# Attention's value rows fetched once on 32 partitions, with GpSimd copying them to the other 96

## The chip, the cores and the metric

The kernel runs on one core of a Trainium2 chip. The metric is the device time of one execution in microseconds (us), the median of several runs. A profile of one further execution shows when each instruction ran on each engine: PE (TensorE, matrix multiplies, with PEld its weight loads), DVE (VectorE), ACT (ScalarE), POOL (GpSimd) and SP (SyncE, which here issues nearly all DMAs). SBUF is the on-chip memory with 128 partitions, PSUM the accumulator memory of PE, DRAM the memory outside.

## What is computed

Attention with a bias that depends on position, followed by a gated feed-forward block, all in float32:

```python
B, H, S, D = q.shape                      # 8, 8, 576, 64
scores = 1/sqrt(D) * q @ k^T + bias       # bias: [H, S, S], a small MLP of the relative position
attn   = softmax(scores)                  # max subtracted, 1e-9 added to the sum
x      = attn @ v                         # then heads side by side: [B*S, H*D] = [4608, 512]
out    = ((x @ w1) * (x @ w2)) @ w3 @ w_out
```

`w3` is 1024 by 1024 and `w_out` 1024 by 512. The inputs of the feed-forward block arrive as 64-bit floats and are converted to float32 on the chip.

## The kernel before

There are three stages. A prologue computes the bias and writes it to DRAM. The attention stage runs from about 60 to 490 us. The feed-forward stage takes the rest.

**Units.** Attention works through 32 units: four pairs of heads times eight batches. For each unit, `op_S` multiplies queries and keys (nine tiles of 128 query rows, L264), `op_T` adds the bias, takes the row extreme and scales on DVE (L275), `op_E` takes the exponential on ACT (L304), `op_R` transposes 32 by 32 blocks on DVE into the tile `pt` (L314), `op_W` multiplies the transposed probabilities with the values (L360), and `op_X` empties PSUM on ACT (L369, L374).

**Why the values stand four times.** A 32-by-32 block transpose leaves the probabilities of a block of 32 keys spread over four groups of 32 partitions, each group holding other query rows. `op_W` therefore contracts over 32 partitions at a time, with `rows = slice(32 * a, 32 * a + 32)` for a = 0 to 3, and needs the same 32 value rows on each of the four groups. Before the change the host repeats them four times in DRAM, and `op_l` (DMA at L252) loads all 128 partitions. A unit's values come as five parts `v0` to `v4` of 4, 4, 3, 4 and 3 key blocks. Each part has one buffer, so part n of the next unit is loaded only after `op_W` of part n in this unit has read it.

**The order of work.** The functions `rhythm` and `arrange` hold a table of times per unit, with a period of 12.17. Work is sorted by these numbers, and this fixes the instruction order on PE, ACT, DVE and POOL. The order on SP's DMA queue is made by the framework's scheduler from the dependences. Every engine executes its own instructions strictly in order, and so does SP: a DMA whose condition is not met holds back all DMAs behind it.

**What else runs beside attention.** In units 1 to 6 of each eight, one block of feed-forward weights is converted, 24 blocks in all, in seven steps `c0` to `c6`: fetch into the tile `wi` (SP, L140), three passes on ACT (`c1` L145, `c2` L149, `c3` L152), a clamp on POOL (`c4`, L155), a shift on DVE (`c5`, L159) and two POOL instructions that put the result together (`c6`, L163 and L164). `wi` has two buffers. The fetch of a later block waits for the L164 that last read its buffer.

In units 2 to 6 of each eight, for the first three pairs of heads, the bias tiles `nb0`, `nb1`, `nb4`, `nb5` and `nbM` of the next pair are loaded from DRAM by `load_bias` (L233; L224 and L225 for `nbM`). POOL first writes zeros to one column of the tile (L230, L223), and the DMA waits for that write.

Of the kernel before, what the change touches and what calls it, by code (L numbers as in the profile page):

```python
# [42 lines left out]
def rhythm(tiles, turns):  # L43

    at = {}
    for n, t in enumerate(tiles):
        at["S" + t] = S_AT[n], "PE"
        at["T" + t] = T_AT[n], "DVE"
        at["E" + t] = E_AT[n], "ACT"
    for n, ts in enumerate(turns):  # L50
        at["R" + ts] = R_AT[n], "DVE"
    at["r"] = PERIOD + 2.62, "DVE"
    at["rd"] = PERIOD + 3.80, "SP"
    for n, w in enumerate(W_AT):
        at[f"W{n}"] = PERIOD + w, "PE"
        at[f"lv{n}"] = w + 1.90, "SP"
    at["X"] = 2 * PERIOD + 1.70, "ACT"
    at["xd"] = 2 * PERIOD + 2.80, "SP"
    for h in range(2):
        for k, n in enumerate("kq"):  # L60
            at[f"l{n}{h}"] = -2 * PERIOD + (5.50, 9.80)[h] + 0.1 * k, "SP"
    at["c0"] = 0.2, "SP"
    at["c1"] = 5.60, "ACT"
    at["c2"] = 8.15, "ACT"
    at["c3"] = 11.65, "ACT"
    at["c4"] = 6.30, "POOL"
    at["c5"] = 9.20, "DVE"
    at["c6"] = 12.40, "POOL"
    return at


def arrange(NU, pieces):

    at = [rhythm(FIRST, ("02", "13", "46", "57", "M"))]
    at += [rhythm(TILES, ("02", "46", "M", "13", "57")) for u in range(1, NU)]
    for k, n in enumerate(("lk0", "lq0")):
        at[2][n] = -2 * PERIOD + 9.60 + 0.1 * k, "SP"
    return {
        (n, u): (u * PERIOD + t + 1.4, e) for u in range(NU) for n, (t, e) in at[u].items() if n[0] != "c" or u in pieces
    }  # L80
# [3 lines left out]
def relpos_attention_moe(  # L84
# [17 lines left out]
    nc = tc.nc  # L102
    NPAIR, B, _, S2 = q.shape
    S, D, H = S2 // 2, P // 2, 2 * NPAIR
# [102 lines left out]
    st = {u: {} for u in range(NU)}  # L207
# [31 lines left out]
    def op_l(u, which):  # L239
        p, b = units[u]  # L240
        n = int(which[1])
        if which[0] == "v":
            b0, b1 = PARTS[n]
            t = vp.tile([P, b1 - b0, 2, D], F32, name=f"v{n}")
            src = v[p, b].rearrange("p (b h d) -> p b h d", h=2, d=D)[:, b0:b1]
            for i in range(b0, b1):
                st[u]["v", i] = t[:, i - b0]
        else:
            w = S if which[0] == "q" else HS
            t = st[u][which] = raw.tile([P, w], F32, name=which)  # L250
            src = {"q": q, "k": k}[which[0]][p, b][:, n * w:(n + 1) * w]
        nc.sync.dma_start(t, src)  # L252

    def op_S(u, t):

        d = st[u]
        s = d["s", t] = ps_s.tile([P, 2, 512], F32, name="s")
        for hf, rows in enumerate((lo, hi)):
            if t == "M":
                parts = [(outs, g, 512, 64) for g, outs in enumerate((lo, hi))]  # L260
            else:
                parts = [(slice(0, P), int(t) % 2, int(t) // 2 * P, P)]
            for outs, h, q0, n in parts:
                nc.tensor.matmul(  # L264
                    s[outs, hf, :HS], d[f"q{h}"][rows, q0:q0 + n],
                    d[f"k{h}"][rows, :], start=True, stop=True,
                )
# [18 lines left out]
    for i in range(2):  # L286
        t = att.enter_context(tc.tile_pool(name=f"sums{i}", bufs=1)).tile([P, 64], F32, name=f"sums{i}")
# [105 lines left out]
    def op_c(u, n):  # L393
        pieces[u][int(n)]()

    made = dict(l=op_l, S=op_S, T=op_T, E=op_E, R=op_R, r=op_r, W=op_W, X=op_X, x=op_x, c=op_c)
    later = []
    for (n, u), (at, on) in arrange(NU, pieces).items():
        step = lambda n=n, u=u: made[n[0]](u, n[1:])
# [13 lines left out]
    with ExitStack() as pro:  # L413
# [29 lines left out]
        def reach(G):  # L443

            return (G + 1) * GR - 1, S - 1 - G * GR
# [9 lines left out]
        for G in range(NGRP):  # L455
            n = max(reach(G)) + 1
# [42 lines left out]
        for G in range(NGRP):  # L499
            at = -LEAD + G * PACE_B  # L500
# [162 lines left out]
    for i in range(2 * NF):  # L663
        at = t_s + AT_F + min(i, N_F) * PACE_F0 + max(i - N_F, 0) * PACE_F
# [11 lines left out]
    for n in range(4, 2 * NF):  # L676
        at = t_s + AT_W1 + PACE_W * n
# [10 lines left out]
    for n in range(NCH * NF):  # L688
        c, ft = divmod(n, NF)
        at = t_f + STEP * n  # L690
# [62 lines left out]
```

## Time and profile before

| | us |
|---|---|
| median of 3 runs (1141.06 to 1141.1) | 1141.07 |
| the profiled execution | 1142.65 |
| its span, first to last instruction | 1140.9 |
| stretch 60 to 480: DVE busy | 392.38 of 420 |
| stretch 60 to 480: PE busy | 385.36 of 420 |
| stretch 60 to 480: ACT busy | 307.75 of 420 |
| stretch 60 to 480: POOL busy | 111.34 of 420 |

In the stretch 60 to 480 the 16 DMA engines are busy 0.71 of the time and move 226 GB/s on average. From 480 us on they are busy 0.18 of the time. Busy times of PE are modelled ends, so a busy PE is not a PE at its peak. A row of the timeline gives start, duration, engine, line, operation and tiles, and in brackets how long the engine was idle before and what ended that. "issue" there means that the engine waited for nothing that the profile shows.

### The profile page before, as it was taken

To read this page: it belongs to the slowest core of one execution; us is meant where nothing else is said; L and a number is where in the kernel's file an instruction comes from. 1 tells how busy PE (TensorE), PEld (TensorE's weight loads), DVE (VectorE), ACT (ScalarE), POOL (GpSimd) and SP (SyncE) were. 2 spreads that over 40 slices of the span, in tenths; PEclk is the share of its full clock that TensorE was granted. 3 is DMA by queue.
4 is the path that set the end of the run, shared out by engine and by line. 5 is a ranking of instruction groups with operands and counts; after the bars stand their busy time and mean duration, and the time that the engine had idled before them with its cause. 6 is when DMAs were issued, how large, how long until landed. Compare 5 with 4: busy or idle time off the path is not lost.

```text
span 1140.9 us, 32065 instructions
## 1 busy us (share of the span) xinstructions
PE 1086.7 (95%) x13696; PEld 801.6 (70%) x13696; DVE 637.3 (56%) x1204; ACT 510.2 (45%) x1111; POOL 179.9 (16%) x167
## 2 busy tenths in 40 slices
PE   7988999899899989898999999999999999999998
PEld 2355666566565655576888888888888888888887
DVE  8999899899998989846552212222131312223111
ACT  7867767677776767656442121121212112121212
POOL 0023303330331133334440000000000000000000
PEclk9989999899999999999999999999999999999999
DMA  8958676786777667455231202021121202110100
GB/s 277 309 186 287 221 233 219 243 260 214 243 252 252 184 206 226 138 147 159 70 115 38 73 23 68 21 72 40 52 59 37 56 19 74 38 38 1 37 1 37
DMA packets 100558, 149.04 MB, mean 131 GB/s; under 512 B 22848, under 2 KB 53696, under 8 KB 100416
## 3 DMA queue, kind: packets, MB, share of 16 engines
q1 hardware_dynamic: 99984, 146.98, 40.7%
q8 instruction: 107, 1.75, 0.6%
q14 instruction: 35, 0.29, 0.1%
q10 hardware_dynamic: 432, 0.02, 0.0%
HBM read 116.93 MB, written 30.03 MB: 129 GB/s over the span
## 4 chain that ended last, share of the span: by engine, by line
PE 71%; DVE 16%; issue 7%; DMA 2%; ACT 2%; SPq 1%; POOL 0%; DVEq 0%; ACTq 0%; POOLq 0%
PE up L623 35%; PE o L648 17%; PE acc L360 8%; DVE pt L314 7%; PE s L264 7%; DVE ts L275 6%; PE bacc L485 3%; PE wacc L582 1%; DVE zdve L471 1%; ACT x L369 1%; DVE mx L275 1%; DMA nb<-nb_d 0%; DMA rb<-r_m 0%; DVE wmag L159 0%; DMA x_d<-x 0%
## 5 line engine op out<-in xcount | busy, mean ns | idle before, releaser
L631 DVE TENSOR_TENSOR g<-up,a 128x512 f32<-128x512 f32 x72 | 49.8, 692 | 343.7 <-PE up L623 343.7
L360 PE MATMUL acc<-pt,v 32*64 32x128 f32 (+1 forms) x9216 | 214.7, 299 | 27.1 <-issue 19.5
L304 ACT ACTIVATE pp<-ts,mx 128x576 f32<-128x576 f32 x256 | 197.0, 770 | 91.0 <-DVE mx L275 89.8
L360 PEld LDWEIGHTS acc<-pt,v 32*64 32x64 f32 x9216 | 162.4, 133 | 95.4 <-issue 64.8
L623 PE MATMUL up<-xh,wl 128*128 128x512 f32 x576 | 225.1, 391 | 0.0
L623 PE MATMUL up<-xl,wh 128*128 128x512 f32 x576 | 225.1, 391 | 0.0
L623 PE MATMUL up<-xh,wh 128*128 128x512 f32 x576 | 225.1, 391 | 0.0
L264 PE MATMUL s<-k,q 64*128 64x288 f32 (+1 forms) x1280 | 200.0, 450 | 10.6 <-DVE mx L275 4.9
L275 DVE CUSTOM_DVE_ANT_0 ts<-s,nb 128x576 f32<-128x576 f32 x256 | 183.2, 739 | 27.4 <-PE s L264 26.6
L648 PE MATMUL o<-w3s,gh 128*128 128x512 f32 x576 | 177.7, 390 | 0.0
L314 DVE STREAM_TRANSPOSE pt<-pp 128x1152 f32<-128x1152 f32 x128 | 175.7, 1373 | 0.0
L628 ACT COPY a<-up 128x512 f32<-128x512 f32 x72 | 42.2, 587 | 263.0 <-PE up L623 263.0
L264 PEld LDWEIGHTS s<-k,q 64*128 64x128 f32 (+1 forms) x1280 | 93.9, 180 | 81.0 <-DVE mx L275 35.6
L623 PEld LDWEIGHTS up<-xl,wh 128*128 128x128 f32 x576 | 108.2, 188 | 23.4
L623 PEld LDWEIGHTS up<-xh,wl 128*128 128x128 f32 x576 | 108.2, 188 | 23.4
L623 PEld LDWEIGHTS up<-xh,wh 128*128 128x128 f32 x576 | 108.2, 188 | 23.3
L648 PEld LDWEIGHTS o<-w3s,gh 128*128 128x128 f32 x576 | 108.1, 188 | 22.9
L634 ACT ACTIVATE gh<-g 128x512 fp32r<-128x512 f32 x72 | 45.5, 632 | 173.7 <-DVE g L631 173.7
L648 PE MATMUL o<-w3s,gl 128*128 128x512 f32 x288 | 112.1, 389 | 0.0
L609 POOL TENSOR_SCALAR xh<-xr 128x512 fp32r<-128x512 f32 x36 | 22.5, 624 | 446.6 <-DVE xr L605 445.7
L155 POOL TENSOR_SCALAR wmag<-wmag 128x512 f32<-128x512 f32 x24 | 46.0, 1915 | 243.3 <-ACT wmag L145 243.3
L637 DVE TENSOR_TENSOR gl<-g,gh 128x512 fp32r<-128x512 f32 x72 | 50.8, 705 | 51.3 <-ACT gh L634 51.2
(68 smaller groups left out, 906.6 us busy)
## 6 DMA issues: line engine op xcount, KB each, us to landing
v<-in_v_dram SPq DMA_DIRECT2D x96, 256.0 KB, 4.5
q<-in_q_dram SPq DMA_DIRECT2D x64, 288.0 KB, 4.7
wi<-in_moe_w_dram SPq DMA_DIRECT2D x32, 512.0 KB, 4.3
v<-in_v_dram SPq DMA_DIRECT2D x64, 192.0 KB, 4.1
nb_d<-bev SPq DMA_DIRECT2D x36, 295.5 KB, 4.8
k<-in_k_dram SPq DMA_DIRECT2D x64, 144.0 KB, 3.7
nb<-nb_d SPq DMA_DIRECT2D x16, 576.0 KB, 5.6
x_d<-x SPq DMA_DIRECT2D x32, 288.0 KB, 5.1
```

The source lines that it names most:

```text
L155: clamps.tensor_scalar(d["mag"], d["mag"], LEAST, MOST, op0=ALU.max, op1=ALU.min)
L264: nc.tensor.matmul(s[outs, hf, :HS], d[f"q{h}"][rows, q0:q0 + n], d[f"k{h}"][rows, :], start=True, stop=True,)
L275: nc.vector.tensor_tensor_reduce(out=halves(ts), in0=d.pop(("s", t))[:, :, :HS], in1=halves(NB[p, t]), op0=ALU.add, op1=ALU.min, scale=-1. ...
L304: nc.scalar.activation(d["p", ps][:, k * S:(k + 1) * S], ts, AF.Exp, bias=mx, scale=-1.0, accum_out=SUMS[u // 4 % 2][:, col:col + 1],)
L314: nc.vector.transpose(o, st[u].pop(("p", ts)))
L360: nc.tensor.matmul(acc[outs, a, c0:c0 + 32 * (t1 - t0)], d["v", b][rows, h], pt_[rows, t0:t1, 32 * b:32 * b + 32], start=(b == 0), stop=(b ...
L623: nc.tensor.matmul(acc, l[:, cc], r, start=(n == 0), stop=(n == 3 * NC - 1))
L628: nc.scalar.copy(a, ps[0])
L631: nc.vector.tensor_tensor(g, ps[1], a, op=ALU.mult)
L634: nc.scalar.activation(gh, g, AF.Copy)
L637: nc.vector.tensor_tensor(gl, g, f(gh), op=ALU.subtract)
L648: nc.tensor.matmul(d["o", t], l[:, sl], folded[ft][:, r], start=(ft == 0 and n == 0), stop=(ft == NF - 1 and n == 2),)
```

## The change

Three things change. The host no longer repeats the value rows four times. `op_l` loads each value part into partitions 0 to 31 only, so that a part of four blocks is 64 KB instead of 256 KB, and one of three blocks 48 KB instead of 192 KB. A new step `op_V` makes two POOL copies per part: partitions 0 to 31 to 32 to 63, then 0 to 63 to 64 to 127. The second copy waits for the first. The table gives `op_V` of part n the time w + 5.50, where w is the part's entry in `W_AT`, and it moves `c5` from 9.20 to 9.30.

```diff
         at[f"lv{n}"] = w + 1.90, "SP"
+        at[f"V{n}"] = w + 5.50, "POOL"
...
-    at["c5"] = 9.20, "DVE"
+    at["c5"] = 9.30, "DVE"
...
             for i in range(b0, b1):
                 st[u]["v", i] = t[:, i - b0]
+            st[u]["vt", n] = t
+            t = t[0:32]
...
         nc.sync.dma_start(t, src)
+
+    def op_V(u, n):
+
+        t = st[u].pop(("vt", int(n)))
+        nc.gpsimd.tensor_copy(t[32:64], t[0:32])
+        nc.gpsimd.tensor_copy(t[64:128], t[0:64])
...
-    inputs["v"] = _np.tile(a.reshape(*a.shape[:3], -1), (1, 1, 4, 1))
+    inputs["v"] = a.reshape(*a.shape[:3], -1)
```

The lines of the changed kernel stand a few lines further down: L155 is L156 there, L159 is L160, L163 and L164 are L164 and L165, L252 is L255, L275 is L284, and the two copies are L260 and L261.

**POOL, third pair of heads, units 2 and 3 of eight.** Before, two clamps (L155) stand with the two closing instructions (L163, L164) between them, and the zero column of `nb1` follows the second clamp:

```order
L155 TENSOR_SCALAR wmag_5253<-wmag_5253 128x512
L163 TENSOR_TENSOR w3s2_70<-w3s2_70,wmag_5253 128x512
L164 TENSOR_TENSOR w3s2_70<-w3s2_70,wi_5251 128x512
L155 TENSOR_SCALAR wmag_5509<-wmag_5509 128x512
L230 MEMSET nb1_5645 128x1
L163 TENSOR_TENSOR w3s3_71<-w3s3_71,wmag_5509 128x512
L164 TENSOR_TENSOR w3s3_71<-w3s3_71,wi_5507 128x512
```

Now, from behind the first of these L164 (and the copies of part 2) on:

```order
L260 COPY v3_5662<-v3_5662 32x512
L261 COPY v3_5662<-v3_5662 64x512
L260 COPY v4_5711<-v4_5711 32x384
L261 COPY v4_5711<-v4_5711 64x384
L156 TENSOR_SCALAR wmag_5693<-wmag_5693 128x512
L231 MEMSET nb1_5835 128x1
L260 COPY v0_5767<-v0_5767 32x512
L261 COPY v0_5767<-v0_5767 64x512
L260 COPY v1_5827<-v1_5827 32x512
L261 COPY v1_5827<-v1_5827 64x512
L164 TENSOR_TENSOR w3s3_71<-w3s3_71,wmag_5693 128x512
L165 TENSOR_TENSOR w3s3_71<-w3s3_71,wi_5691 128x512
```

The clamp now stands behind the copies of parts 3 and 4, and the closing pair stands behind those of parts 0 and 1.

**DVE, at the shift `c5` of the next unit.** `ppM` is the ninth tile of probabilities, the odd one. Before:

```order
L275 ISA ts_5935,mx_5936<-s_5904,nb5_4179 128x576
L275 ISA mx_5936 128x1
L159 TENSOR_SCALAR wmag_5765<-wmag_5765 128x512
L314 STREAM_TRANSPOSE pt0_841<-ppM_5893 128x576
L275 ISA ts_5955,mx_5956<-s_5939,nb5_4179 128x576
```

Now:

```order
L284 ISA ts_6137,mx_6138<-s_6104,nb5_4311 128x576
L284 ISA mx_6138 128x1
L323 STREAM_TRANSPOSE pt0_841<-ppM_6093 128x576
L160 TENSOR_SCALAR wmag_5959<-wmag_5959 128x512
L284 ISA ts_6157,mx_6158<-s_6141,nb5_4311 128x576
```

The shift and the transpose of `ppM` have changed places. Nothing else moves on DVE, and PE and ACT keep their order.

**SP, third pair of heads, units 5 and 6.** Before, the loads of `nb5` and `nbM` (two DMAs) stand ahead of `v0` and of the fetch of `wi`:

```order
L233 DMA nb5_6211<-nb_d_87 128x2x576
L252 DMA v0_6097<-in_v_dram 128x512
L252 DMA k0_6106<-in_k_dram 128x288
L252 DMA q0_6141<-in_q_dram 128x576
L252 DMA v1_6155<-in_v_dram 128x512
L252 DMA v2_6204<-in_v_dram 128x384
L252 DMA k1_6202<-in_k_dram 128x288
L252 DMA q1_6206<-in_q_dram 128x576
L224 DMA nbM_6362<-nb_d_87 64x576
L225 DMA nbM_6362<-nb_d_87 64x576
L140 DMA wi_7032<-in_moe_w3_dram 128x1024
L252 DMA v3_6252<-in_v_dram 128x512
```

Now:

```order
L234 DMA nb5_6423<-nb_d_87 128x2x576
L255 DMA v1_6365<-in_v_dram 32x512
L255 DMA v2_6416<-in_v_dram 32x384
L255 DMA k1_6414<-in_k_dram 128x288
L255 DMA q1_6418<-in_q_dram 128x576
L141 DMA wi_7276<-in_moe_w3_dram 128x1024
L255 DMA v3_6466<-in_v_dram 32x512
L225 DMA nbM_6580<-nb_d_87 64x576
L255 DMA v4_6515<-in_v_dram 32x384
L389 DMA x_d2_90<-x_6511 128x576
L226 DMA nbM_6580<-nb_d_87 64x576
```

`nb5` has moved behind `v0`, `k0` and `q0`, to just ahead of `v1`. The first half of `nbM` now stands between `v3` and `v4`. Its zero column stands between the copies of those two parts on POOL, as that of `nb5` stands between the copies of parts 0 and 1.

More of the change, by code (lines that the diff above doesn't have):

```diff
@@ L394, in op_c @@
         pieces[u][int(n)]()
-    made = dict(l=op_l, S=op_S, T=op_T, E=op_E, R=op_R, r=op_r, W=op_W, X=op_X, x=op_x, c=op_c)
+    made = dict(l=op_l, S=op_S, V=op_V, T=op_T, E=op_E, R=op_R, r=op_r, W=op_W, X=op_X, x=op_x, c=op_c)
     later = []
```

## The prediction

> **What bounds the kernel now.** I read the page by stage first, then the groups of instructions in the attention stage (60 to 480 us), then the timelines of POOL, DVE and SP there.
>
> ```profile
> span 1140.9 us, 32065 instructions
> ...
> DVE  8999899899998989846552212222131312223111
> POOL 0023303330331133334440000000000000000000
> ...
> q1 hardware_dynamic: 99984, 146.98, 40.7%
> q8 instruction: 107, 1.75, 0.6%
> ```
> ```profile
> L275 DVE CUSTOM_DVE_ANT_0 ts<-s,nb 128x576 f32<-128x576 f32 x250 | 178.8, 739 | 24.7 <-PE s L264 24.5
> ...
> L275 DVE CUSTOM_DVE_ANT_0 ts<-s,nbM 128x576 f32<-128x576 f32 x32 | 23.1, 722 | 1.3 <-PE s L264 1.3
> ```
>
> The change touches attention alone, the first 17 slices, where DVE is at 8 or 9 tenths. DVE sets the pace. It loses 24.7 + 1.3 = 26 us, all of it waiting for scores from PE. That is all that a calmer stage could give back. How long a unit takes undisturbed is read from POOL and DVE around the first converting units of the third pair of heads:
>
> ```profile
> 282.67 1.91 POOL L155 TENSOR_SCALAR wmag<-wmag 128x512 f32<-128x512 f32 x1 [30.02 <-ACT wmag L145]
> 286.71 1.27 POOL L163 TENSOR_TENSOR w3s<-w3s,wmag 128x512 int32<-128x512 int32 x1 [2.12 <-DMA v<-in_v_dram]
> 289.52 1.29 POOL L164 TENSOR_TENSOR w3s<-w3s,wi 128x512 f32<-128x512 f32 x1 [1.54 <-issue]
> ...
> 294.87 1.92 POOL L155 TENSOR_SCALAR wmag<-wmag 128x512 f32<-128x512 f32 x1 [4.02 <-ACT wmag L145]
> 298.89 1.28 POOL L163 TENSOR_TENSOR w3s<-w3s,wmag 128x512 int32<-128x512 int32 x1 [2.11 <-DVE wmag L159]
> 301.69 1.29 POOL L164 TENSOR_TENSOR w3s<-w3s,wi 128x512 f32<-128x512 f32 x1 [1.52 <-issue]
> ```
> ```profile
> 298.32 0.42 DVE L159 TENSOR_SCALAR wmag<-wmag 128x512 int32<-128x512 int32 x1
> 298.66 0.77 DVE L314 STREAM_TRANSPOSE pt<-ppM 128x576 f32<-128x576 f32 x1
> 299.35 0.72 DVE L275 CUSTOM_DVE_ANT_0 ts<-s,nb 128x576 f32<-128x576 f32 x1
> ```
>
> From clamp to clamp it is 294.87 - 282.67 = 12.20 us. POOL works some 4.5 us of that and rests. The clamp ends at 296.79, and DVE takes its shift (L159) at 298.32, so nothing waits for POOL. With the shift behind the transpose of ppM, as now, the clamp may end at 299.01 (298.32 plus the 0.69 from 298.66 to 299.35) before DVE stalls. The third view is SP's issues:
>
> ```profile
> 290.87 0.38 SPq L233 DMA_DIRECT2D nb<-nb_d  x1
> 291.35 0.41 SPq L140 DMA_DIRECT2D wi<-in_moe_w_dram  x1
> 291.85 0.86 SPq L252 DMA_DIRECT2D v<-in_v_dram  x2
> ...
> 303.01 0.33 SPq L140 DMA_DIRECT2D wi<-in_moe_w_dram  x1
> 303.43 0.86 SPq L252 DMA_DIRECT2D v<-in_v_dram  x2
> ...
> 309.02 0.38 SPq L233 DMA_DIRECT2D nb<-nb_d  x1
> 309.49 0.42 SPq L252 DMA_DIRECT2D v<-in_v_dram  x1
> ...
> 310.95 0.38 SPq L252 DMA_DIRECT2D v<-in_v_dram  x1
> ```
>
> L164 ends at 302.98 and the fetch of wi goes out at 303.01, with v3 and v4 right behind it. SP stood waiting for POOL. Issue to landing, by tile, in this order: wi of 303.01, v of 291.85, v of 309.49, v of 310.95, all v of the run, all wi from 60 to 470 us:
>
> ```profile
> DMA to landing us min/median/max: 3.9/3.9/3.9
> DMA to landing us min/median/max: 6.0/6.0/6.0
> DMA to landing us min/median/max: 3.9/3.9/3.9
> DMA to landing us min/median/max: 5.6/5.6/5.6
> DMA to landing us min/median/max: 2.3/4.3/7.1
> DMA to landing us min/median/max: 3.4/4.4/6.2
> ```
>
> **What the change removes.** A unit's values shrink from 1152 to 288 KB, over 32 units 28 of q1's 147 MB. That can pay only through the 26 us above. Part of those are waits of PE that end in "issue":
>
> ```profile
> L360 PE MATMUL acc<-pt,v 32*64 32x128 f32 (+1 forms) x9021 | 209.5, 298 | 24.4 <-issue 16.7 <-ACT x L374 7.5
> ...
> PE 1086.7 (95%) x13696; PEld 801.6 (70%) x13696; DVE 637.3 (56%) x1204; ACT 510.2 (45%) x1111; POOL 179.9 (16%) x167
> ```
>
> The two counts of 13696 are 27392 instructions, 256 for each of q8's 107 packets of 16 KB. I take these waits to be PE's own instructions arriving late behind data in the DMA engines. Fewer bytes shorten them. I credit the change with all 26 us, less 1 that may stay.
>
> **What it adds: the price of a copy.** No row shows a POOL copy. The nearest:
>
> ```profile
> masks.py:197 POOL MEMSET ident<- 128x128 f32 x1 | 0.2, 204 | 0.3 <-POOLq L738 0.3
> L288 POOL MEMSET sums<- 128x64 f32 x2 | 0.2, 152 | 0.0
> L609 POOL TENSOR_SCALAR xh<-xr 128x512 fp32r<-128x512 f32 x36 | 22.5, 624 | 446.6 <-DVE xr L605 445.7 <-DMA rb<-r_m 1.0
> L164 POOL TENSOR_TENSOR w3s<-w3s,wi 128x512 f32<-128x512 f32 x16 | 20.7, 1293 | 32.7 <-issue 27.6 <-DMA v<-in_v_dram 3.6 <-DVE pt L314 1.5
> ```
>
> The two memsets give 52 ns for 64 elements, 0.81 ns each, and 100 ns fixed: 0.52 us for 512 if reading is free, 0.41 for 384. The scalar pass reads one input and does two operations in 0.624 (scaled, 0.49 for 384). A copy lies between; I take 0.57 and 0.45. The far end is the two-input 1.29. A copy here also shifts partitions, which no row shows. The handover between dependent POOL instructions:
>
> ```profile
> 480.52 1.27 POOL L163 TENSOR_TENSOR w<-w,wmag 128x512 int32<-128x512 int32 x1
> 481.86 1.62 POOL L164 TENSOR_TENSOR w<-w,wi 128x512 f32<-128x512 f32 x1
> ```
>
> That is 481.86 - 481.79 = 0.07, or 0.1 with a start from a semaphore. So a part of 512 costs 2 x 0.57 + 0.1 = 1.24 us, one of 384 1.00. A unit's five parts cost 5.7, and with the 4.5 above POOL has 10.2 of work in 12.2. By sums it fits.
>
> [...]
>
> **What it moves: a ring through POOL, SP and DMA.** By the order, the clamp now stands behind the copies of v3 and v4. These wait for DMAs that SP issues only behind the wi fetch, which waits for the previous L164. L164 in turn stands behind the copies of v0 and v1, and those behind the clamp. What lay side by side is now one ring. From the end of L164 (zero):
> - wi is issued at once and lands at 3.9. v3 and v4 (112 KB) are right behind it, so 4.0. Bounds: 3.5, from wi's shortest landing of 3.4, and 4.6.
> - Copies of v3 and v4: 1.24 + 1.00, to 6.24. The clamp, 1.92, to 8.16.
> - Copies of v0 and v1 (landed by then): 2.48. L163, 0.07 and L164: 1.27 + 0.07 + 1.29 = 2.63. End: **13.27**, against 12.20.
>
> The clamp gates DVE's shift, and behind that in DVE's queue stand all further bias additions and transposes. So a late ring stalls DVE, and PE and ACT after it. Units that also load bias are worse, because a zero column stands between copies and SP's queue waits for it:
>
> ```profile
> SPq L233 <- POOL nb L230: 39.7, 12, 4.8
> ```
>
> - Unit 2 (nb0 ahead of wi): today v of 291.85 lands 7.0 after nb's issue, behind 1344 KB. Now 1152 KB, some 6.2. Ring: 6.2 + 2.24 + 1.92 + 2.48 + 2.63 = 15.5.
> - Unit 3 (nb1 behind the clamp, v0 and v1 behind nb1): nb1 goes out at 8.4. v1 landed 7.5 after nb with 1520 KB; with 1136 KB, 5.7, so 14.1. Copy 1.24, closing 2.63: 18.0. DMA latency is paid twice.
> - Unit 4 (nb4 between wi and v3, 1.25 late): v3 at 6.2 as in unit 2, 15.5.
> - Unit 5 (nb5 behind the copies of v0, ahead of v1): nb5 out at 9.6. Today v0 lands 4.4 after nb with 832 KB; with 640 KB, 4.0, so 13.6. Then 1.24 + 2.63: 17.5.
> - Unit 6 (nbM between v3 and v4): v3's copies end at 5.24, nbM and v4 go out by 5.9. v4 lands 3.0 later (between 2.3 and 4.3). Copies 1.00, clamp 1.92: clamp ends at 11.8.
>
> From L164 of unit 1 (ends 290.81, as today) to the clamp of unit 6: 15.5 + 18.0 + 15.5 + 17.5 + 11.8 = 78.3 us. Free of charge are 299.01 + 4 x 12.20 - 290.81 = 57.0. DVE stalls 21.3 per pair of heads, 64 for the three that load bias. The last pair: 4 x 13.27 + 8.16 - 57.0 = 4.2. **Sum:** 1140.9 + 64 + 4 - 26 + 1 = 1184. The median of the runs (1141.07) stands 0.2 over the span, the profiled execution (1142.65) 1.75 over it; I give the median as **1184**.
>
> Ends: with copies of 0.52 and 0.41 and landings 0.5 shorter (1 us where bias is ahead), a round is 12.4, the three pairs lose 15 each and the last none: +19, so 1160. With 0.62 and 0.49 and landings 0.6 longer, a round is 14.2, the stalls 27 each and 9: +65, so 1206. The shift may cost more too, since it now runs beside copies:
>
> ```profile
> L159 DVE TENSOR_SCALAR wmag<-wmag x12: 416/424/1420, 500.7 to 577.9; 128x512 int32<-128x512 int32 x12
> ```
>
> That row is from the later stage, where POOL is often busy; at 1.0 more in 24 units it is 24 us at most. I take 0, as DVE is waiting there anyway. [...]
>
> **The rivals.**
> - *The ring fits* (8%). If v3 lands within 2.9 us of L164 and the bias loads find as much slack, a round is 12.2 and only the shorter waits count, of which I leave 5: 1141 - 26 + 5 = 1120. For it: DMA loses a quarter of its bytes in this stage. Against it: wi alone, 512 KB ahead of v3, never landed under 3.4.
> - *The ring holds, but bias loads don't lengthen it* (12%). If SP's wait is absorbed by the slack of the values, all four pairs cost 4: 1141 + 17 - 26 + 1 = 1133. Against it: the order shows v0 and v1 behind nb1.
> - *Copies at the two-input price* (5%). With 1.29 and 0.98 a round is 18.6 and POOL is the bound: 45 to 50 per pair, 28 in the last: 1141 + 143 + 28 - 26 = some 1285.
> - *Bytes that were hidden anyway* (5%): stalls and gains balance within 2 us, 1141.
>
> **How the numbers follow.** The forecast has 70%, its own range 1160 to 1206. The rivals on the fast side hold 20%, of which I count 3 as no change. Faster by over 0.2% (2.3 us, what a measurement here tells from none) 17%, within it 8%, slower 75%. For 8 in 10, the range runs from the second rival to just above the forecast's end: 1132 to 1208.
>
> **What would show it.** Right: the shift on DVE is the stalled instruction, released by POOL's clamp, with some 60 to 70 us in all; clamps in units 2 to 6 stand 15 to 18 us apart; POOL's copies wait for DMA of v; PE's "issue" waits shrink. Wrong at the price: copies outside 0.5 to 0.65 us. Wrong at the ring: the wi fetch, v3 and clamp in a row take under 7 us. If DVE's idle time is below 26 us, the whole argument falls.

## The result and the profile after

| | before | after |
|---|---|---|
| median of the runs, us | 1141.07 (6 runs, 1133.36 to 1147.55) | 1205.61 (6 runs, 1203.08 to 1207.53) |
| the profiled execution, us | 1142.65 | 1204.01 |
| its span, us | 1140.9 | 1202.2 |

The ratio of the times is 1.0566, with a 95% interval of 1.0526 to 1.0606. The change makes the kernel 64.5 us slower. That is the forecast's direction, 22 us above its number and just inside its range, whose upper end is 1206. The page of the changed kernel, with the same rows as before:

```profile
span 1202.2 us, 32561 instructions
...
DVE  8898769866986699895655131312232222223111
POOL 6845665665565557785434000000000000000000
...
q1 hardware_dynamic: 84624, 118.67, 31.8%
```

The bytes went as announced, 147 to 119 MB on q1. But DVE's row in the attention stage now has sixes and sevens where it had eights and nines. What DVE waited for, in groups of instructions from 60 to 560 us (after the second bar: idle time just before, and what ended it):

```profile
L284 DVE CUSTOM_DVE_ANT_0 ts<-s,nb 128x576 f32<-128x576 f32 x250 | 179.1, 740 | 6.0 <-PE s L273 5.2
...
L284 DVE CUSTOM_DVE_ANT_0 ts<-s,nbM 128x576 f32<-128x576 f32 x32 | 23.1, 722 | 2.3 <-PE s L273 2.2
L160 DVE TENSOR_SCALAR wmag<-wmag 128x512 int32<-128x512 int32 x26 | 11.9, 459 | 78.0 <-POOL wmag L156 72.2 <-POOL nb L231 5.7
```

The waits for scores fell from 26 to 7.4 us. In their place stands one new wait, 78.0 us at the shift (L160) for POOL. 78.0 less the 18.6 saved is 59.4 of the 61.3 us by which the span grew. What comes behind attention is no longer than before: from the last start of L369 (L360 before) to the end it is 647.6 us against 647.2. PE's granted clock fell in the stretch 60 to 480, to 0.91 from 0.97, but DVE waits less for PE there than before, so the lower clock is not what made it slow. The same group of the shift, asked for the four pairs of heads one after the other (60 to 178, 178 to 304, 304 to 425 and 425 to 560 us):

```profile
L160 DVE TENSOR_SCALAR wmag<-wmag 128x512 int32<-128x512 int32 x6 | 2.9, 482 | 24.1 <-POOL wmag L156 22.1 <-POOL nb L231 2.0
L160 DVE TENSOR_SCALAR wmag<-wmag 128x512 int32<-128x512 int32 x6 | 2.8, 466 | 27.0 <-POOL wmag L156 25.3 <-POOL nb L231 1.7
L160 DVE TENSOR_SCALAR wmag<-wmag 128x512 int32<-128x512 int32 x6 | 2.6, 434 | 22.4 <-POOL wmag L156 20.4 <-POOL nb L231 1.9
L160 DVE TENSOR_SCALAR wmag<-wmag 128x512 int32<-128x512 int32 x8 | 3.6, 456 | 4.5 <-POOL wmag L156 4.4
```

The three pairs that load bias pay 22 to 27 us each, the last one 4.5. The engines in between show why: POOL waits for values, and SP, which fetches them, waits for POOL (rows of the waits: us in total, times, longest):

```profile
POOL v L260 <- DMA v<-in_v_dram: 146.0, 51, 10.2
```
```profile
SPq L141 <- POOL w3s L165: 80.5, 13, 8.2
...
SPq L141 <- POOL wos L165: 40.7, 6, 8.1
...
SPq L234 <- POOL nb L231: 51.5, 12, 7.2
...
SPq L225 <- POOL nbM L224: 14.2, 3, 5.2
```

SP stands 187 us behind POOL here, against 83 for the same lines before (25.4 + 10.8 + 39.7 + 7.5). One round of the third pair in POOL's timeline, from the end of one L165 (349.11 + 1.29 = 350.40) to the end of the next (370.54):

```profile
349.11 1.29 POOL L165 TENSOR_TENSOR w3s<-w3s,wi 128x512 f32<-128x512 f32 x1
...
354.82 0.61 POOL L260 COPY v<-v 32x512 f32<-32x512 f32 x1 [3.29 <-DMA v<-in_v_dram]
355.49 0.61 POOL L261 COPY v<-v 64x512 f32<-64x512 f32 x1
...
357.31 1.92 POOL L156 TENSOR_SCALAR wmag<-wmag 128x512 f32<-128x512 f32 x1
359.17 0.10 POOL L231 MEMSET nb<- 128x1 f32 x1
364.79 0.60 POOL L260 COPY v<-v 32x512 f32<-32x512 f32 x1 [5.52 <-DMA v<-in_v_dram]
...
366.56 0.61 POOL L260 COPY v<-v 32x512 f32<-32x512 f32 x1 [0.49 <-DMA v<-in_v_dram]
...
367.92 1.26 POOL L164 TENSOR_TENSOR w3s<-w3s,wmag 128x512 int32<-128x512 int32 x1
369.26 1.28 POOL L165 TENSOR_TENSOR w3s<-w3s,wi 128x512 f32<-128x512 f32 x1
```
```profile
350.43 0.33 SPq L141 DMA_DIRECT2D wi<-in_moe_w_dram  x1
350.85 1.71 SPq L255 DMA_DIRECT2D v<-in_v_dram  x2
...
359.30 0.39 SPq L234 DMA_DIRECT2D nb<-nb_d  x1
359.78 1.40 SPq L255 DMA_DIRECT2D v<-in_v_dram  x1
```

Each link of the ring can be seen. SP's fetch of `wi` goes out 0.03 us after L165 ends, and v3 and v4 behind it. Their copies begin at 354.82, the clamp stands behind them, the zero column behind the clamp, the load of `nb1` 0.03 us behind the column, v0 and v1 behind that load, and L164 and L165 behind their copies. This round pays the latency of a transfer twice and takes 20.1 us. The same round took 19.8 and 18.6 us in the first two pairs.

### The profile page after: what moved, and what is told of

It reads as the page before. It is cut to its first block, busy times and chain, and to the rows that moved or that the text cites. A ratio compares the mean times of both kernels' runs of the same rounds, so it can differ in the third digit from the quotient of the medians.

```text
span 1202.2 us, 32561 instructions
## 1 busy us (share of the span) xinstructions
PE 1106.7 (92%) x13696; PEld 810.4 (67%) x13696; DVE 640.9 (53%) x1204; ACT 511.0 (43%) x1111; POOL 405.4 (34%) x487
## 4 chain that ended last, share of the span: by engine, by line
PE 58%; DVE 13%; POOL 11%; DMA 10%; issue 5%; ACT 2%; SPq 1%; POOLq 0%; DVEq 0%; ACTq 0%
PE up L632 33%; PE o L657 16%; DMA v<-in_v_dram 8%; DVE pt L323 5%; DVE ts L284 5%; POOL wmag L156 3%; PE acc L369 3%; PE s L273 3%; POOL v L260 3%; POOL v L261 3%; PE bacc L494 2%; PE wacc L591 1%; POOL w3s L165 1%; DMA nb<-nb_d 1%; DVE mx L284 0%
## 5 line engine op out<-in xcount | busy, mean ns | idle before, releaser
L369 PE MATMUL acc<-pt,v 32*64 32x128 f32 (+1 forms) x9216 | 227.8, 306 | 29.4 <-DMA v<-in_v_dram 12.3
L273 PE MATMUL s<-k,q 64*128 64x288 f32 (+1 forms) x1280 | 206.9, 464 | 47.4 <-DVE mx L284 46.9
L369 PEld LDWEIGHTS acc<-pt,v 32*64 32x64 f32 x9216 | 169.6, 137 | 105.3 <-issue 44.8
L260 POOL COPY v<-v 32x512 f32<-32x512 f32 (+1 forms) x160 | 133.5, 834 | 175.4 <-DMA v<-in_v_dram 146.0
L284 DVE CUSTOM_DVE_ANT_0 ts<-s,nb 128x576 f32<-128x576 f32 x256 | 183.5, 741 | 9.5 <-PE s L273 7.3
L261 POOL COPY v<-v 64x512 f32<-64x512 f32 (+1 forms) x160 | 91.3, 571 | 9.8
```

The costliest lines, as they stand in the source:

```text
L260: nc.gpsimd.tensor_copy(t[32:64], t[0:32])
L261: nc.gpsimd.tensor_copy(t[64:128], t[0:64])
L273: nc.tensor.matmul(s[outs, hf, :HS], d[f"q{h}"][rows, q0:q0 + n], d[f"k{h}"][rows, :], start=True, stop=True,)
L284: nc.vector.tensor_tensor_reduce(out=halves(ts), in0=d.pop(("s", t))[:, :, :HS], in1=halves(NB[p, t]), op0=ALU.add, op1=ALU.min, scale=-1. ...
L369: nc.tensor.matmul(acc[outs, a, c0:c0 + 32 * (t1 - t0)], d["v", b][rows, h], pt_[rows, t0:t1, 32 * b:32 * b + 32], start=(b == 0), stop=(b ...
```

## The experiments

Theory: the ring. POOL's order and SP's two waits for POOL (the weight fetch behind L165, the bias loads behind the zero columns) are one closed loop, and this loop sets the pace. The rivals are the price of POOL's copies (the engine is too full, or the copies hold up DVE), the 32-partition DMAs (slower than full ones), and POOL's order by itself. All comparisons are with runs of the kernel before on the same chip, median 1140.9 to 1144.7 us. Line numbers are those of the changed kernel unless the kernel before is named; without copies the bias addition is L289.

### The clamp ahead of two copies

```diff
-        at[f"V{n}"] = w + 5.50, "POOL"
+        at[f"V{n}"] = (w + 5.50, PERIOD + 6.40 + 0.05 * n)[n > 2], "POOL"
```

> POOL's order alone is changed: the copies of parts 3 and 4 stand behind the clamp instead of ahead of it. Ring theory (the clamp waits for the DMAs of v3 and v4, and DVE's shift waits for the clamp): DVE's wait for POOL's clamp, 72 us in the changed kernel, falls below 15 us, the last pair of heads loses nothing, and the bias units still lose some 6 us per pair, now by PE waiting for copies: about 1153 us (1140 to 1168). [...]

Measured: 1168.65 us, ratio 1.0236 (1.0181 to 1.0291). The stalls at the shift fell to 7.8 us, but another wait came up. The waits, and the group of the bias addition from 60 to 560 us:

```profile
PEld acc L369 <- DMA v<-in_v_dram: 28.4, 15, 4.6
...
DVE wmag L160 <- POOL wmag L156: 7.8, 6, 1.7
```
```profile
L284 DVE CUSTOM_DVE_ANT_0 ts<-s,nb 128x576 f32<-128x576 f32 x249 | 178.5, 738 | 44.3 <-PE s L273 44.0
```

So the clamp's place sets where DVE stalls. It does not open the ring: SP still waits for POOL, the values come late, and now PE waits for them at L369 and is late with the scores that stand behind in its order. The expectation held in the stalls. It had put some 6 us per pair on PE waiting for copies, 18 in all, where DVE now waits 44 for scores, so its time was 16 us too low and the result stands just above its range.

### Zero columns on DVE

```diff
-                nc.gpsimd.memset(nb[:, 0:1], 0.0)
+                nc.vector.memset(nb[:, 0:1], 0.0)
...
-            nc.gpsimd.memset(nb[:, 0, 0:1], 0.0)
+            nc.vector.memset(nb[:, 0, 0:1], 0.0)
```

> The zero columns of the bias tiles are written by DVE instead of POOL, so that SP's bias loads no longer wait for POOL. Ring theory: the bias units fall back to the plain round of about 14.2 us, the first three pairs of heads lose 4 to 8 us each instead of 22 to 27, the last one 4 as now: about 1150 us (1142 to 1162). Rival, the rounds are long because POOL has too much to do: the fifteen 0.1 us writes matter nothing, 1205.

Measured: 1158.49 us, ratio 1.0165 (1.0115 to 1.0215). The waits:

```profile
DVE wmag L160 <- POOL wmag L156: 32.8, 18, 4.2
DVE ts L284 <- PE s L273: 7.2, 10, 1.9
```

Taking 15 memsets of 0.1 us off POOL gave 47 us (1205.61 to 1158.49). The groups by pair have stalls of 10.5, 10.0, 8.8 and 3.7 us, where they had 24.1, 27.0, 22.4 and 4.5. So the extra that the bias loads cost is mostly gone, and the plain ring through the weight fetch is left.

### The weight fetch on ACT's queue

```diff
-    at["c0"] = 0.2, "SP"
+    at["c0"] = 9.5 - PERIOD, "ACT"
...
-        return narrow(cva, moe_w3[ft * P:(ft + 1) * P, cs], 512, w3s[ft][:, cs], nc.sync, clamps=nc.gpsimd)
+        return narrow(cva, moe_w3[ft * P:(ft + 1) * P, cs], 512, w3s[ft][:, cs], nc.scalar, clamps=nc.gpsimd)
```

The same for `w_out`.

> The changed kernel with one edit: the fetch of the expert weights (L141) is issued from ACT's queue instead of SP's, so that SP no longer stands behind the narrowing on POOL (L165) before it can fetch a part of the values. If the ring of the prediction (POOL's narrowing, SP's weight fetch, SP's value fetch, POOL's copies, POOL's clamp) is what makes the rounds long, the last pair, which has no bias loads, loses its stall of 4.4 us at the shift (L160) and its rounds fall from 14.4 to 12.2 us, and groups 1 to 3 keep part of theirs, since their bias loads still stand on SP behind POOL's zero columns (L224, L231): stalls of 40 to 60 us instead of 78, and 1165 us (1150 to 1190). If SP only happens to be late and POOL's own work is what sets the rounds, the stalls stay near 78 and the time stays at 1200 to 1210.

Measured: 1174.15 us, ratio 1.0262 (1.0219 to 1.0305). The shift in the last pair (420 to 560 us), and SP's waits:

```profile
L160 DVE TENSOR_SCALAR wmag<-wmag 128x512 int32<-128x512 int32 x13 | 6.2, 476 | 0.1
```
```profile
SPq L234 <- POOL nb L231: 59.7, 12, 7.6
...
SPq L225 <- POOL nbM L224: 28.5, 3, 10.7
```

The last pair, which loads no bias, loses its stall. The other three keep 40.2 us, through the zero columns. This is the other half of the ring, as foreseen.

### Both waits of SP cut

Both edits together, POOL's order and copies as in the changed kernel.

> The changed kernel with two edits: the zero columns on DVE and the weight fetch on ACT's queue; the copies of parts 3 and 4 stay ahead of the clamp (L156). SP then waits for no work of POOL in either kind of round, but POOL's clamp still stands behind two pairs of copies and behind the landing of parts 3 and 4. If the loss needs SP's wait as well as POOL's order (a closed ring), the stalls at the shift (L160) fall below 5 us and the time is that of all three edits, 1121 us (1115 to 1130). If the order on POOL alone delays the clamp, stalls of 10 to 30 us stay, and the time is 1130 to 1150.

Measured: 1118.91 us, ratio 0.9809 (0.9764 to 0.9853). The shift, and what POOL waited for:

```profile
L160 DVE TENSOR_SCALAR wmag<-wmag 128x512 int32<-128x512 int32 x38 | 20.5, 540 | 0.3
```
```profile
POOL v L260 <- DMA v<-in_v_dram: 73.8, 49, 10.1
```

This run decides. POOL does the same copies in the same order, still ahead of the clamp, and still waits 73.8 us for values, but the stalls are 0.3 us and the span is 1117.3. So neither the price of the copies nor POOL's order alone made the kernel slow. The closed loop through SP did, and each of its two paths carries part of it: with one cut, 33 or 40 us of stalls are left, with both none. The edit to the weight fetch takes away SP's wait and, with it, the 512 KB that stood ahead of v3 and v4; how much of the gain belongs to each was not separated.

### The clamp first as well

The clamp ahead of two copies with the zero columns on DVE, and then with all three edits:

> The changed kernel with two edits together: POOL copies parts 3 and 4 after its clamp of the round (L156) instead of before it, and DVE sets the zero columns (L224, L231) in place of POOL, so that the bias loads on SP stand behind nothing of POOL. If the two orders on POOL account for the loss, the stalls at the shift go from 78 us to under 5, and the 44 us in which DVE waited for scores when the clamp alone was put first shrink with the shorter rounds to 10 to 20: 1130 us (1118 to 1145), faster than before. If the late copies of parts 3 and 4 by themselves starve PE's weighted sums (L369), the waits for scores stay near 40 us and the time is 1150 to 1165.

> The changed kernel with all three edits: the copies of parts 3 and 4 behind the clamp, the zero columns on DVE, the weight fetch on ACT's queue. Nothing of the ring is left: SP waits for no work of POOL but for free buffers. By the theory of the ring the kernel keeps the 25 us that loading a quarter of the values gave by itself (1116 us without copies), less what the copies cost beside DVE's shifts: 1120 us (1114 to 1135). If POOL's copies themselves hold DVE up or POOL is simply too full, the time stays above 1141.

Measured: 1134.3 us, ratio 0.9936 (0.9894 to 0.9977), and 1121.06 us, ratio 0.9803 (0.9764 to 0.9842). The stalls are 0.2 and 0.3 us. Putting the clamp first adds nothing once SP waits for neither kind of POOL's work: 1121.06 with it against 1118.91 without.

### The load alone and the copies alone

The first run loads 32 partitions and makes no copies (one buffer for each part, filled once on the other 96 partitions, so it leaves out the right values there). The second loads all 128 partitions as before and makes the copies as well.

> Left out: the copies. Values are loaded on 32 partitions, and the other 96 keep the values of the first unit, so three quarters of the value rows are stale. This is the gain alone. My prediction credited 25 us: 1116. From the changed kernel's profile, where DVE's waits for scores fell from 26 to 7 but other stalls may cover some: 1116 to 1125. Rival, the bytes were hidden anyway: 1139 to 1143.

> Values are loaded on all 128 partitions as before the change, and the copies run on top of them. Ring theory: the same ring, with 448 KB instead of 112 KB behind the weight block, so 0.6 to 1 us more per round, and PE's late instructions back: 1225 us (1210 to 1245). Rival, the loss comes from DMAs that write only 32 partitions: 1141 to 1155.

Measured: 1116.12 us, ratio 0.9791 (0.9746 to 0.9835), and 1230.98 us, ratio 1.0788 (1.0736 to 1.084). DVE's bias addition without copies, and its shift with full loads and copies, from 60 to 560 us:

```profile
L289 DVE CUSTOM_DVE_ANT_0 ts<-s,nb 128x576 f32<-128x576 f32 x249 | 177.9, 740 | 7.0 <-PE s L278 6.9
```
```profile
L160 DVE TENSOR_SCALAR wmag<-wmag 128x512 int32<-128x512 int32 x24 | 11.0, 457 | 96.5 <-POOL wmag L156 86.8 <-POOL nb L231 9.8
```

Loads on 32 partitions are not the trouble: alone they give 25 us. With full loads the same ring turns more slowly, with 96.5 us of stalls in place of 78.0.

### The kernel before with the two edits

> The kernel before with the same two edits, zero columns on DVE and weight fetch on ACT's queue, and no other change: values still come from DRAM on all 128 partitions. If the gain of the version with all edits (1121 us) comes from loading a quarter of the values, this one keeps the 26 us in which DVE waits for scores and stays at 1141 us (1135 to 1146). If the looser queues alone are what gains, it comes out at 1120 to 1130.

Measured: 1118.78 us, ratio 0.9815 (0.9772 to 0.9859). The expectation's first branch, that the bytes are what gains, fell; the time stands 1.2 us below the range of the second. The kernel before gains 22 us from the two queue edits, with all its bytes. The waits of the whole run, first in the kernel before, then with the two edits, and the stretch from 60 to 480 us with the two edits (busy time of PE, PEld, DVE, ACT and POOL, clock, DMA share, GB/s):

```profile
PEld acc L360 <- issue: 64.8, 119, 3.0
...
DVE ts L275 <- PE s L264: 28.0, 27, 2.5
```
```profile
PEld acc L360 <- issue: 51.1, 112, 2.8
PEld s L264 <- issue: 30.7, 115, 0.5
...
DVE ts L275 <- PE s L264: 9.4, 12, 1.9
```
```profile
60.00:480.00 420.00, 395.71 (x10537) 258.66 (x10538) 399.82 (x803) 317.17 (x758) 119.40 (x82) 0.99 0.73 232
```

The waits for scores fell from 28.0 to 9.4 us while the DMA engines were busier, 0.73 of the stretch and 232 GB/s against 0.71 and 226 before. So the mean load alone does not make the scores late. It also follows that with these two edits the quarter-size load, together with its copies, brings nothing that can be measured: 1118.91 us with it, 1118.78 without. Two more runs part the edits:

> The kernel before with one of the two edits alone: the zero columns on DVE, so that the bias loads on SP wait for nothing of POOL. In the kernel before SP stood 47 us behind those columns and 36 us behind POOL's narrowing of the weights, and both edits together brought the kernel before to 1118.8 us. If it is SP's standing still, after which loads go out in a bunch ahead of PE's instructions, that makes DVE wait for scores, this edit takes a good half of the 22 us: 1128 us (1122 to 1134), the waits for scores down from 28 to about 17 us. If it is the place and queue of the 512 KB weight fetch that matters, it stays at 1137 to 1142.

> The kernel before with the other edit alone: the weight fetch on ACT's queue. By SP's standing still it takes a little less than half of the 22 us: 1131 us (1125 to 1137). If the place and queue of the 512 KB weight fetch are what matters, it gains nearly all: 1118 to 1124, with the waits for scores down to about 9 us.

Measured: 1139.73 us, ratio 0.9984 (0.9953 to 1.0016), for the zero columns, and 1124.74 us, ratio 0.9857 (0.9794 to 0.9921), for the fetch. DVE's wait in the two, in this order (the second execution profiled, with a span of 1129.8 us, was slower than the median):

```profile
DVE ts L275 <- PE s L264: 26.7, 29, 2.6
```
```profile
DVE ts L275 <- PE s L264: 18.0, 18, 3.3
```

The zero columns alone give nothing that can be told from the noise, the weight fetch's place and queue give most of it: 17.7 us. By the theory that SP's standing still makes the scores late in proportion to its length, the zero columns should have given the larger part, and that is not what came. The fetch's 1124.74 lies just outside both ranges given for it. The test is weaker than it was planned, though. With the columns on DVE, SP stood 61.9 us behind L164 (39.6 + 22.3) where it had stood 36.2, so only 21.5 of the 83.4 us went away; with the fetch on ACT's queue 39.3 were left at the bias loads (L233).

The edit gives the fetch another queue and another place in the table, 9.5 - 12.17 for 0.2, and these two were not separated. On the chip the fetch did not come earlier by this. On SP's queue it goes out as soon as an L164 has freed its buffer, long before it is needed: the fetch of 303.01 in the kernel before goes out 0.03 us after that L164 ends and is first read by ACT (L145) at 321.80, 18.8 us later, and that of 350.43 in the changed kernel (L146) at 367.32. On ACT's queue, in the kernel before with both edits, the fetch below goes out, by estimate, some 7 us after that L164, and so waits for nothing of POOL. The estimate takes this block's L145 on ACT, at 286.07, and the 8.9 us from L145 to the end of L164 in the kernel before (281.92 to 290.81).

```profile
301.98 0.37 ACTq L140 DMA_DIRECT2D wi<-in_moe_w_dram  x1
```

ACT first reads this one at 311.21, 9.2 us later. So SP stood waiting in order to send early what was not needed early.

### What holds POOL's first copy

The first copy of the run took 39.27 us in the changed kernel, and 38.87 in the version with all three edits. In that version the prologue's passes on DVE were changed from one tensor and a constant to two tensors:

```diff
-                nc.vector.tensor_scalar(
-                    z[:, 0:n], tsh[:, 0:n], beta[:, grp:grp + 1], 0.0, op0=ALU.add, op1=ALU.max,
+                nc.vector.scalar_tensor_tensor(
+                    z[:, 0:n], tsh[:, 0:n], beta[:, grp:grp + 1], zero[:, 0:n], op0=ALU.add, op1=ALU.max,
```

> The version with all three edits, with one more: in the prologue DVE makes its passes over the bias network (L480) from two tensors, adding the column and taking the maximum with a tensor of zeros, in place of the one-tensor form with the constant 0. The first copy of the values (L260) took 38.87 us beside DVE's one-tensor passes and ended 0.1 to 0.5 us after the last of them. If it is DVE's one-tensor form that keeps POOL from its memory, the copy takes about 0.6 us here (up to 1.5), while DVE's passes get longer, from 486 ns to about 690 for 512 elements, and the prologue by some 15 us. If any back-to-back work of DVE on SBUF keeps POOL out, or the copy waited for something else in the prologue, it stays over 30 us.

Measured, with one run: 1147.93 us. POOL and DVE in the timeline:

```profile
12.05 67.79 POOL L260 COPY v<-v 32x512 f32<-32x512 f32 x1 [10.11 <-DMA v<-in_v_dram]
79.90 0.61 POOL L261 COPY v<-v 64x512 f32<-64x512 f32 x1
```
```profile
69.43 9.94 DVE L482 SCALAR_TENSOR_TENSOR zdve<-tsh,beta,zero 128x512 f32<-128x512 f32 x14
```

The one-tensor form is not the cause by itself. The passes got longer (one of 512 elements now 756 ns on average, 486 before) and the copy got longer with them: it ended at 79.84, 0.47 us after DVE's last pass at 79.37. Something else that ends with these passes is not excluded; no run has the copy without them.

## Why the prediction was right, and where its sizes were off

**DVE sets the pace, and the shift stalls.** Right, as the 78.0 us show. The forecast had 68. One sign was put wrongly: the clamps do not stand 15 to 18 us apart but by turns some 14 and some 22 (14.5, 22.1, 14.0 and 22.5 in the third pair). It is the rounds, from one L165 to the next, that take 16.4 to 20.1 us there.

**The ring.** Right, and shown by cutting SP's two waits. The links of the round shown above, from the end of an L165: values of the plain link copied from 4.4 (354.82 - 350.40; forecast 4.0), clamp ended at 8.8 (8.16), bias load out at 8.9 (8.4), v1 landed at 16.2 (14.1), round closed at 20.1 (18.0). Behind the bias load v1 landed 7.3 us after the load's issue, not 5.7. Scaling the landing with the bytes was not at fault there: from its own issue v1 landed in 4.2 us, where it had taken 5.6 before. But SP's issue of v0 took 1.40 us instead of 0.42, so v1's went out 1.0 later than forecast. In the other two pairs the same stretch was 7.1 and 5.9 us.

The terms were short in every kind of round that loads bias. Units 2 to 5 took 16.8, 19.5, 17.1 and 19.4 us on average over the three pairs, where 15.5, 18.0, 15.5 and 17.5 were forecast. Of these 1.3 to 1.9 us, about 0.35 is the price of eight copies and, in all but unit 3, 0.25 a copy that runs beside the shift. Most of the rest is values that came later than estimated. From L165 of unit 1 to the clamp of unit 6 the pairs took 83.9, 86.8 and 83.8 us, not 78.3.

**The price of a copy.** Mis-sized by 0.04 to 0.06 us. The groups of copies on POOL:

```profile
L261 POOL COPY v<-v 64x512 f32<-64x512 f32 x96 | 59.1, 615 | 5.9
...
L260 POOL COPY v<-v 32x384 f32<-32x384 f32 x64 | 32.5, 508 | 22.4 <-DMA v<-in_v_dram 16.1 <-PE acc L369 3.0
```

It is 0.61 us for 512 elements and 0.50 for 384, whether 32 or 64 partitions are written, where 0.57 and 0.45 were taken. The scalar pass over one input, with two operations, at 0.624 was the nearer row. The forecast's upper end of 1206 us, with copies of 0.62 and 0.49 and landings 0.6 longer, is where the result stands. Undisturbed copies of 512 stand at 0.60 to 0.61 in the timeline.

**The gain.** The forecast credited 25 us. The load alone gave it (1140.9 to 1116.1). In the changed kernel 18.6 us showed, and 7.4 us of waits for scores remained beside the stalls. The step's reason was too narrow, however. "Fewer bytes shorten them" holds: PE's waits that end in "issue" fell from 118 to 79 us in the changed kernel, and with both queue edits they are 92 us with all bytes and 69 with a quarter. But DVE's waits for scores shrink almost as far with all bytes and the two queue edits (9.4 us) as with the small load alone (10.5). That PE's instructions come late because the DMA engines are loaded was argued, and the busier engines of the run that had shorter waits speak against the mean load as the only reason. What exactly delays PE stays open.

**The sum.** The span is 18.3 us above the forecast's 1183.9 (1140.9 + 64 + 4 - 26 + 1, rounded to 1184 there): 78.0 - 68 = 10 from the stalls, 25 - 18.6 = 6.4 from the gain, and 2 that no single row carries. The median stands 3.4 us over the span of the profiled execution where the forecast set 0.2.

**The shift beside copies.** Taken at nothing, and it was little: 471 ns in the stretch 60 to 480 of the changed kernel, against 422 before. With the stalls gone it costs 540 ns from 60 to 560 us in the version with both queue edits, against 458 in the kernel before with these edits, 3 us over 38 shifts.

**The rivals.** Copies at the price of two inputs: ruled out by the 0.61. Bytes hidden anyway, and a ring that fits: ruled out as the kernel was built, but a ring that no longer binds is what two queue edits make of it, and their 1118.91 is near the 1120 given for the second. Bias loads that don't lengthen the ring: the run with zero columns on DVE shows that they cost 47 us.

## What to carry to other kernels

Before work is put on an engine with much free time, ask in which order it then stands there, who waits for what is behind it, and whether that wait leads back to the new work. An engine half idle can still close a loop, and then the latencies in the loop set the pace, not the sums of work: here POOL was busy 240.87 of the 420 us from 60 to 480, and DVE's shift stalled for 78.0 us in all. And before bytes are cut to shorten a wait, look for a transfer on the same queue that waits for something and is not needed soon, and move it to another queue or another time: here the weight fetch alone gave 18 us, with the zero columns 22, where cutting the values to a quarter gave 25.

## What the runs showed of the hardware

The first copy on POOL stood for 39.27 us, until DVE's passes in the prologue were done. This copy in the changed kernel, the next one, and DVE's passes in the same stretch:

```profile
11.58 39.27 POOL L260 COPY v<-v 32x512 f32<-32x512 f32 x1 [10.16 <-DMA v<-in_v_dram]
50.91 0.61 POOL L261 COPY v<-v 64x512 f32<-64x512 f32 x1
```
```profile
5.24 45.14 DVE L480 TENSOR_SCALAR zdve<-tsh,beta 128x576 f32<-128x576 f32 x126
```

The copy ended at 50.85, 0.47 us after the last pass at 50.38, the same 0.47 as beside the two-tensor passes. DVE was not slowed: its 126 passes took 45.14 us before as well, and its first bias addition started at 52.33 against 52.56. Nothing needed the copy sooner, since PE first reads values (L369) at 68.4. In attention a copy of 512 elements that starts with DVE's shift takes 0.86 us instead of 0.61, as here, and 0.86 or 0.87 in all 12 such copies from 60 to 480 us:

```profile
344.80 0.86 POOL L260 COPY v<-v 32x512 f32<-32x512 f32 x1
```
```profile
344.77 0.43 DVE L160 TENSOR_SCALAR wmag<-wmag 128x512 int32<-128x512 int32 x1 [2.56 <-POOL wmag L156]
```

This copy ends at 345.66, 0.46 us after the shift's end at 345.20.

What held the copies is not shown: the trace gives no reason for a long copy. It shows the two forms of passes, with copies of 39.27 and 67.79 us that both ended 0.47 us after the last pass. The bias additions and the transposes, 155.5 and 149.5 us for the full tiles among the 337.99 that DVE was busy from 60 to 480 us, left the copies at 0.61 us: the one of 345.72 took 0.61 beside a bias addition (345.11, 0.75 us) and a transpose (345.79, 1.37 us).
